# Pooled attention with a gated MLP on one core: a new order of issue for the stretch ahead of the repeated part, and a 1e-9 added by GpSimd

## The chip, the core and the metric

The kernel runs on one core of a Trainium2 chip. The metric is device time in microseconds (us). The kernel before was timed three times: the median is 588.71 us, the lowest 588.38 us and the highest 590.66 us. GB/s and MB are decimal; KB in the table of DMA issues is 1024 bytes.

## The reference

There are 8 batches of 576 rows, 8 heads of 64. Attention runs against keys and values that are pooled by 8 (72 of each), and its output goes into a gated MLP with a spatial gate over the 576 rows.

```python
k_p = k.reshape(B, H, Sp, pool, D).mean(axis=3)      # Sp = 72, pool = 8
v_p = v.reshape(B, H, Sp, pool, D).mean(axis=3)
scores = scale * np.matmul(q, k_p.transpose(0, 1, 3, 2))
scores = scores - np.max(scores, axis=-1, keepdims=True)
attn = np.exp(scores)
attn = attn / (np.sum(attn, axis=-1, keepdims=True) + 1e-09)
x = np.matmul(attn, v_p)                             # heads side by side: 576 x 512
h = gelu(x @ w_in);  u, v = halves of h              # w_in 512 x 1024, tanh form of gelu
v_n = layer_norm(v) * g_ln
gated = u * (einsum('ts,bsd->btd', w_sg, v_n) + b_sg)
out = x + gated @ w_out
```

The weights w_in and w_out arrive as 64-bit floats and are turned into 32-bit ones in the kernel. The large products run as three passes on fp32r halves (high by high, low by high, high by low).

## The kernel before

The work of a batch is cut into steps. A letter names a step, a digit its part, and each step is a generator that issues some instructions and then yields. A token such as `S0+1` advances step S, part 0, of the batch that lies one after the current one, up to its next yield. `PROLOGUE` (lines 23 to 38) is the list of tokens that fills the pipeline, with batches counted from 0. `PERIOD` (lines 39 to 47) is the repeated part: it is emitted for b = 1 to 10 and holds every step once, spread over several batches. `emit` (line 699) walks these lists, so each engine's queue holds its instructions in the order in which the tokens emit them. Lines 710 to 715 then pin that order for each engine. SyncE (SP) issues almost all DMAs, in token order too, and every engine takes its queue strictly in order.

The steps, with the parts that matter here:

- A and B load keys and values of half the heads into `kvraw` (batch 0's values go to `early`), E loads what is left over of both (`left`), C loads the queries of one pair of heads (`early` and `qraw` for batch 0, `qraw` afterwards).
- K pools the keys. For batch 0 TensorE does it, with matmuls by the identity; from batch 1 on VectorE (DVE) does it, with one TENSOR_REDUCE at line 313 per load. K2 pools the left-over rows (`lp`, DVE), transposes on TensorE and writes the block-diagonal `kbd` (ScalarE, lines 343 and 344). P does the same for the values (`vp`, `vb`, `vbh`, `vbl`, `vl`).
- Q turns the queries into `qT`: through TensorE and ScalarE for batch 0, by a DVE STREAM_TRANSPOSE (line 410) later.
- S is the softmax of one pair of heads. TensorE writes the scores to PSUM (`mps` for batch 0, `aps` later, two buffers each); DVE takes the maximum (`nmax`, line 427). From there the softmax has two forms. The short one: ScalarE takes ten exponentials with the bias and the sum in the same instruction (line 444), DVE adds 1e-9 (line 451). The long one, chosen by the tuple `SOFTMAX` at line 75 for six pairs of batches 0 and 1: DVE subtracts the maximum (line 437), ScalarE takes one exponential of all 720 values a row (line 439), DVE sums (line 447) and adds 1e-9 (line 448). Both end with RECIPROCAL (line 454) and a product (line 455) on DVE. GpSimd (POOL) then copies the left-over columns to `el` (line 461).
- T and L transpose the attention weights and the left-over columns (`e`, `el`) and copy them to `ah`, `al` and `lt`; in L the copies for the two halves of the heads alternate between ScalarE (lines 475 and 476) and DVE (line 478). V multiplies by the pooled values, ScalarE writes `x` and `xhl`'s high half (lines 520 and 521), POOL its low half (line 523).
- H and U are the two halves of x @ w_in, W the spatial gate, O the output product, Z the output's transpose and its stores.
- `lv`, `lu`, `lo`, `ls` load the weights; `v`, `u`, `o`, `s` prepare one part of them each. A part of w_in or w_out costs two ScalarE instructions (lines 194 and 195), two of DVE (197 and 198), one of POOL (200), one of ScalarE (203) and one of POOL (205). A part of w_sg costs a transpose on TensorE, a cast on ScalarE and a subtraction on DVE (line 158, `wsl`).

The lines of the long softmax that the change touches, and the end that both forms share:

```python
        if mode:
            yield
            nc.vector.tensor_reduce(out=ssum, in_=e, axis=AX.X, op=ALU.add)
            nc.vector.tensor_scalar(ssum, ssum, 1e-9, None, op0=ALU.add)
        else:
            yield
            nc.vector.tensor_scalar(ssum, ssum, 1e-9, None, op0=ALU.add)

        rec = flat[:, 0:SLOT * NT].rearrange("p (s k) -> p s k", k=SLOT)[:, :, 2 * SP:2 * SP + 2]
        nc.vector.reciprocal(rec, ssum)
```

Of the kernel before, what the change touches and what calls it, by code (L numbers as in the profile page):

```python
# [20 lines left out]


PROLOGUE = """
A0+0 K0+0 A1+0 C0+0 K1+0 E0+0 lv0 K0+0 C1+0 K2+0 K1+0 K2+0 Q0+0 Q1+0 B0+0 C2+0 K2+0 A1+1 Q0+0 v1 v1 v1 S0+0 C3+0 S0+0
v0 Q1+0 S0+0 v0 B1+0 S1+0 S1+0 S1+0 Q2+0 Q3+0 S1+0 S0+0 Q2+0 v1 lv1 S0+0 Q3+0 v0 S2+0 T0+0 ls0 S1+0 v0 A0+1 S2+0 v1
S3+0 K1+1 E0+1 S3+0 T0+0 S2+0 v0 S3+0 S2+0 S3+0 P1+0 B1+1 S1+0 lu0 v3 P0+0 s3 S2+0 S3+0 T1+0 P2+0 v3 S3+0 s1 C0+1 v2
K0+1 T1+0 B0+1 L0+0 L0+0 v3 s3 C1+1 s1 v3 V0+0 K2+1 lo0 s3 V0+0 v2 V1+0 V1+0 s1 s2 T3+0 T2+0 T3+0 s4 v3 T2+0 v2 u1
V0+0 K2+1 P1+1 Q0+1 u1 K2+1 V1+0 v2 P0+1 u1 V3+0 s2 Q1+1 V3+0 V3+0 V2+0 V2+0 S0+1 v2 s2 C3+1 s4 V0+0 u1 S0+1 V3+0
S0+1 S0+1 u0 S1+1 V2+0 s4 lu1 H2+0 C2+1 S1+1 S1+1 u1 S0+1 u0 S1+1 H0+0 T0+1 H2+0 S1+1 H0+0 u3 Q3+1 u0 P2+1 s0 A1+2
V2+0 U1+0 u3 s0 V1+0 u3 s0 S3+1 u3 H1+0 U1+0 u0 Q2+1 H2+0 T0+1 S3+1 H0+0 H4+0 H2+0 u0 T0+1 H2+0 H2+0 H0+0 S2+1 S0+1  # L30
u2 C0+2 H1+0 H4+0 U0+0 S3+1 H1+0 S2+1 S3+1 H4+0 u3 S2+1 H0+0 u2 S2+1 S3+1 u2 U0+0 u2 H3+0 A0+2 H4+0 o1 H0+0 H3+0 S2+1
u2 o0 H1+0 S3+1 U3+0 H4+0 C1+2 H1+0 H3+0 U2+0 S2+1 P2+1 H4+0 H3+0 U3+0 lo1 P2+1 H4+0 o0 S1+1 L0+1 H1+0 H4+0 H3+0 P2+1
L0+1 L0+1 H3+0 L0+1 o0 U2+0 o0 Q0+2 W2+0 T1+1 V0+1 T1+1 o0 W0+0 o1 K0+2 o1 V0+1 o2 o1 T1+1 V1+1 E0+2 T2+1 W2+0 o1
T2+1 o2 W3+0 o2 W0+0 T2+1 o3 o2 o3 o3 V1+1 V2+1 K1+2 T3+1 V1+1 Q1+2 V2+1 T3+1 W1+0 W0+0 K2+2 o3 W2+0 K2+2 W0+0 T3+1
V3+1 W3+0 W1+0 C2+2 W2+0 K2+2 S0+2 V3+1 S1+2 B0+2 W1+0 S0+2 W3+0 Q2+2 W1+0 W3+0 O0+0 B1+2 V1+1 P1+2 P0+2 S1+2 o2 S0+2
V0+1 S1+2 C3+2 O1+0 O0+0 V2+1 S0+2 S0+2 O0+0 Z0+0 V3+1 O1+0 o3 S2+2 S2+2 P2+2 A0+3 O1+0 H2+1 S1+2 O2+0 Z1+0 O2+0 S2+2
A1+3 Q3+2 T0+2 Z0+0 V3+1 O2+0 H2+1 C0+3
""".split()
# [12 lines left out]
def tile_pooled_attn_gmlp(ctx: ExitStack, tc: tile.TileContext, q, k, v, w_in, g_ln, w_sg, b_sg, w_out, out):  # L51
    nc = tc.nc
# [361 lines left out]
    def step_S(b, g):  # L414
# [30 lines left out]
        if mode:  # L445
            yield
            nc.vector.tensor_reduce(out=ssum, in_=e, axis=AX.X, op=ALU.add)
            nc.vector.tensor_scalar(ssum, ssum, 1e-9, None, op0=ALU.add)
        else:
            yield  # L450
            nc.vector.tensor_scalar(ssum, ssum, 1e-9, None, op0=ALU.add)
# [288 lines left out]
```

## Time and profile before

| | value |
|---|---|
| median of 3 runs | 588.71 us (588.38 to 590.66) |
| the profiled execution's own time | 589.3 us |
| its span, first to last instruction | 587.6 us |
| TensorE (PE) busy | 558.1 us (95%) |
| DVE busy | 411.6 us (70%) |
| ScalarE (ACT) busy | 349.2 us (59%) |
| POOL busy | 220.7 us (38%) |
| mean granted TensorE clock | 0.982 |

Busy time is the sum of an engine's instructions; PE's matmuls are pipelined. Idle time is put down to the event that came last before the engine went on. Rows of the timeline give the start in us, the length in us, the engine, line, operation and tiles, and in square brackets how long the engine sat idle ahead of it and who released it.

### The profile page before, as it was taken

What the parts mean: (1) busy time and instruction counts of PE and PEld (TensorE: products, weight loads), DVE (VectorE), ACT (ScalarE), POOL (GpSimd) and SP (SyncE); (2) the same over time, 40 slices, a digit from 0 to 9 for tenths busy, and PEclk for the clock granted to TensorE, in tenths of its full rate; (3) what the DMA queues carried; (4) which work ended last, traced back from release to release, by engine and by line L of the source; (5) the groups of instructions that cost most, each with busy time, mean ns of one, the idle gap of its engine ahead of it and who ended that gap; (6) DMA issues with size and microseconds to landing.
All of it is one profiled execution on the core that took longest, in us unless ns stands there. A gap on an engine that the chain in (4) does not pass through costs nothing.

```text
span 587.6 us, 10312 instructions
## 1 busy us (share of the span) xinstructions
PE 558.1 (95%) x3793; PEld 527.3 (90%) x3793; DVE 411.6 (70%) x562; ACT 349.2 (59%) x981; POOL 220.7 (38%) x295
## 2 busy tenths in 40 slices
PE   4687997999999999999999999999999999999995
PEld 4675886999999989999999989999999989998995
DVE  1688998997758786787758786787758765444434
ACT  1686784797556775577556775577556775412310
POOL 3337366572407032342407032442407032433230
PEclk9699998999999999999999999999999999999998
DMA  8999651453351733124351634125350211021105
GB/s 213 217 225 197 156 130 27 94 101 64 67 106 37 110 63 86 32 59 94 67 105 37 108 67 95 21 57 98 67 105 1 42 21 21 1 42 21 20 1 82
DMA packets 161282, 46.34 MB, mean 79 GB/s; under 512 B 148752, under 2 KB 148752, under 8 KB 161232
## 3 DMA queue, kind: packets, MB, share of 16 engines
q1 hardware_dynamic: 156464, 45.10, 38.6%
q10 hardware_dynamic: 4768, 0.59, 0.7%
q8 instruction: 30, 0.49, 0.4%
q14 instruction: 20, 0.16, 0.1%
HBM read 36.23 MB, written 9.44 MB: 78 GB/s over the span
## 4 chain that ended last, share of the span: by engine, by line
PE 79%; DVE 7%; DMA 7%; SPq 3%; issue 1%; POOL 1%; ACT 1%; DVEq 0%
PE mps L99 65%; PE aps L99 10%; PE aps L133 3%; SPq L153 3%; DMA qraw<-in_q 2%; DMA stage<-in_moe_w_sg 2%; DMA left<-in_v 1%; DMA raw<-in_moe_w_in 1%; DVE kp L313 1%; DMA kvraw<-in_k 1%; DVE top L198 1%; DVE mps L612 1%; DVE qT L410 0%; DVE bst L565 0%; DVE u L614 0%
## 5 line engine op out<-in xcount | busy, mean ns | idle before, releaser
L99 PE MATMUL mps<-xhl,wih 128*128 128x288 f32 x512 | 89.9, 298 | 0.1
L623 POOL TENSOR_TENSOR glo<-u,ghi 128x576 fp32r<-128x576 f32 x32 | 45.2, 1426 | 112.1 <-ACT ghi L621 111.2
L99 PE MATMUL mps<-wih,xhl 128*128 128x512 f32 x256 | 86.6, 404 | 0.1
L99 PEld LDWEIGHTS mps<-xhl,wih 128*128 128x128 f32 x512 | 75.8, 188 | 1.8 <-ACT vg L561 0.3
L444 ACT ACTIVATE e<-aps,nmax 128x72 f32<-128x72 f32 x240 | 73.3, 350 | 0.6 <-DVE nmax L427 0.3
L612 DVE SCALAR_TENSOR_TENSOR mps<-mps,gcol,bbc 128x576 f32<-128x576 f32 x32 | 26.4, 825 | 51.2 <-PE mps L99 51.2
L99 PEld LDWEIGHTS mps<-wih,xhl 128*128 128x128 f32 x256 | 48.8, 190 | 11.0 <-DVE x L655 0.3
L444 ACT ACTIVATION_READ_ACCUMULATOR e<-aps,nmax 128x1 f32 x240 | 56.5, 236 | 0.0
L99 PE MATMUL mps<-wsh,vhh 128*128 128x288 f32 x256 | 56.2, 301 | 0.0
L99 PE MATMUL mps<-wsh,vhl 128*128 128x288 f32 x256 | 55.4, 298 | 0.0
L99 PE MATMUL mps<-xhl,wil 128*128 128x288 f32 x256 | 55.0, 296 | 0.0
L99 PE MATMUL mps<-wsl,vhh 128*128 128x288 f32 x256 | 55.0, 296 | 0.0
L571 DVE TENSOR_SCALAR vg<-vg,mv,rstd 128x512 f32<-128x512 f32 (+1 forms) x40 | 40.4, 1011 | 19.4 <-POOL rstd L569 19.3
L523 POOL TENSOR_TENSOR xhl<-x,xhl 128x576 fp32r<-128x576 f32 x32 | 45.3, 1428 | 21.8 <-ACT xhl L521 21.8
L99 PE MATMUL mps<-ghi,woh 128*128 128x288 f32 x240 | 52.6, 300 | 0.0
L568 POOL TENSOR_TENSOR rstd<-mv,eps 128x1 f32<-128x1 f32 (+1 forms) x40 | 10.8, 271 | 110.3 <-DVE mv L566 100.9
L99 PE MATMUL mps<-glo,woh 128*128 128x288 f32 x240 | 51.4, 295 | 0.1
L99 PE MATMUL mps<-wil,xhl 128*128 128x512 f32 x128 | 51.5, 402 | 0.0
L99 PE MATMUL mps<-ghi,wol 128*128 128x288 f32 x240 | 51.3, 295 | 0.0
L561 ACT ACTIVATE vg<-mps 128x512 f32<-128x512 f32 x32 | 19.1, 597 | 48.4 <-PE mps L99 46.5
L581 POOL TENSOR_TENSOR vhl<-vg,vhh 128x512 fp32r<-128x512 f32 x32 | 42.3, 1324 | 7.8 <-ACT vhh L579 7.7
L621 ACT CAST ghi<-u 128x576 fp32r<-128x576 f32 x32 | 21.4, 673 | 37.7 <-DVE u L614 37.7
(157 smaller groups left out, 1428.0 us busy)
## 6 DMA issues: line engine op xcount, KB each, us to landing
out<-y SPq DMA_DIRECT2D x118, 72.0 KB
kvraw<-in_k SPq DMA_DIRECT2D x32, 256.0 KB
...
kvraw<-in_v SPq DMA_DIRECT2D x28, 256.0 KB
...
```

The lines of the kernel that those rows point to most:

```text
L99: nc.tensor.matmul(o, lhsT, rhs, start=start, stop=stop)
L133: nc.tensor.transpose(ps[:rows, i * P:(i + 1) * P], src(i), ident if i < NT - 1 else swap)
L153: queue.dma_start(o, i)
L444: nc.scalar.activation(e[:, i, h], slots[i][:, h], AF.Exp, bias=nmax[:, i, h:h + 1], **acc)
L523: (nc.vector if b in LO_DVE else nc.gpsimd).tensor_tensor(xhl[:, 1, g], x32[:, g], xhl[:, 0, g].bitcast(F32), op=ALU.subtract)
L561: nc.scalar.activation(vg, o, AF.Gelu_apprx_tanh)
L568: nc.gpsimd.tensor_tensor(rstd, mv[:, 1:2], eps[:n, 1:2], op=ALU.add)
L571: nc.vector.tensor_scalar(vg, vg, mv[:, 0:1], rstd, op0=ALU.subtract, op1=ALU.mult)
L581: (nc.gpsimd if i < NT - 1 else nc.vector).tensor_tensor(lo, vg, hi.bitcast(F32), op=ALU.subtract)
L612: nc.vector.scalar_tensor_tensor(vs, vs, gcol[:, d:d + 1], bbc.rearrange("p (a n) -> p a n", a=2), op0=ALU.mult, op1=ALU.add)
L621: nc.scalar.copy(ghi[:, d], uf)
L623: nc.gpsimd.tensor_tensor(glo[:, d], uf, ghi[:, d].bitcast(F32), op=ALU.subtract)
```

## The change

The diff has two parts.

First, `PROLOGUE` is written anew; `PERIOD` and all steps but one stay as they are. The same steps are emitted, in another order. Its first two lines before and after:

```diff
-A0+0 K0+0 A1+0 C0+0 K1+0 E0+0 lv0 K0+0 C1+0 K2+0 K1+0 K2+0 Q0+0 Q1+0 B0+0 C2+0 K2+0 A1+1 Q0+0 v1 v1 v1 S0+0 C3+0 S0+0
+A1+0 A0+0 lv0 v1 E0+0 v1 K0+0 C0+0 v0 K0+0 K2+0 C1+0 K1+0 C2+0 Q0+0 K1+0 K2+0 Q1+0 v0 Q0+0 K2+0 C3+0 S0+0 v1 v0 lv1
...
```

Second, the long softmax. The pair (0, 1) leaves the tuple and takes the short form, and in the five that remain the 1e-9 is added by POOL from a small constant tile, in a step of its own, so that other work can be put between the sum, the addition and the reciprocal:

```diff
-    SOFTMAX = ((0, 1), (0, 3), (1, 0), (1, 1), (1, 2), (1, 3))
+    SOFTMAX = ((0, 3), (1, 0), (1, 1), (1, 2), (1, 3))
...
+    tiny = const.tile([P, NT, 2], F32, name="tiny")
+    nc.gpsimd.memset(tiny, 1e-9)
...
             nc.vector.tensor_reduce(out=ssum, in_=e, axis=AX.X, op=ALU.add)
-            nc.vector.tensor_scalar(ssum, ssum, 1e-9, None, op0=ALU.add)
+            yield
+            nc.gpsimd.tensor_tensor(ssum, ssum, tiny, op=ALU.add)
+            yield
```

Line numbers below 107 stay, those up to the softmax move by 2, those behind it by 4.

Three places show what the new list does to the queues. The first is SP's queue, from the loads of the spatial gate's bias on; `left`, `kvraw` and `qraw` are batch 1's, `raw` is a weight. Before:

```order
L153 DMA gcol_105<-in_moe_g_ln 128x4x1
L153 DMA kvraw_292<-in_k 64x2x512 x2
L153 DMA left_306<-in_k 32x1x512 x2
L153 DMA left_306<-in_v 32x1x512 x2
L153 DMA kvraw_344<-in_v 64x2x512 x2
L153 DMA raw_349<-in_moe_w_in 128x4x512
L153 DMA qraw_393<-in_q 32x18x32 x4
L153 DMA kvraw_404<-in_v 64x2x512 x2
L153 DMA qraw_417<-in_q 32x18x32 x4
L153 DMA raw_430<-in_moe_w_out 128x4x512
```

SP's queue at the same place after the change:

```order
L155 DMA gcol_107<-in_moe_g_ln 128x4x1
L155 DMA left_265<-in_k 32x1x512 x2
L155 DMA left_265<-in_v 32x1x512 x2
L155 DMA kvraw_292<-in_k 64x2x512 x2
L155 DMA raw_346<-in_moe_w_in 128x4x512
L155 DMA kvraw_358<-in_k 64x2x512 x2
L155 DMA qraw_406<-in_q 32x18x32 x4
L155 DMA qraw_427<-in_q 32x18x32 x4
L155 DMA kvraw_437<-in_v 64x2x512 x2
L155 DMA raw_442<-in_moe_w_out 128x4x512
L155 DMA raw_508<-in_moe_w_in 128x4x512
L155 DMA kvraw_678<-in_v 64x2x512 x2
```

Both loads of batch 1's values stood ahead of its second load of queries and now stand behind it, the second of them behind two more weights. The second load of batch 1's keys, which stood ahead of the spatial gate's weights, now stands behind them.

The second place is DVE's queue where batch 1's first two softmaxes (`e_538`, `e_575`) run. Before:

```order
L427 TENSOR_REDUCE nmax_573<-aps_545 128x10
L437 TENSOR_TENSOR e_575<-aps_545,nmax_573 128x720
L447 TENSOR_REDUCE ssum_539<-e_538 128x10
L448 TENSOR_SCALAR ssum_539<-ssum_539 128x10
L454 RECIPROCAL aps_518<-ssum_539 128x5x2
L455 TENSOR_TENSOR e_538<-e_538,aps_518 128x720
L197 TENSOR_SCALAR top_542<-top_542 128x512
L198 SCALAR_TENSOR_TENSOR top_542<-raw_349,top_542 128x512
L447 TENSOR_REDUCE ssum_576<-e_575 128x10
L448 TENSOR_SCALAR ssum_576<-ssum_576 128x10
L454 RECIPROCAL aps_545<-ssum_576 128x5x2
L455 TENSOR_TENSOR e_575<-e_575,aps_545 128x720
```

DVE's queue at the same place after the change, where the two softmaxes are `e_540` and `e_558`:

```order
L429 TENSOR_REDUCE nmax_554<-aps_543 128x10
L439 TENSOR_TENSOR e_558<-aps_543,nmax_554 128x720
L449 TENSOR_REDUCE ssum_541<-e_540 128x10
L315 TENSOR_REDUCE vp_595<-kvraw_437 128x128
L458 RECIPROCAL aps_532<-ssum_541 128x5x2
L459 TENSOR_TENSOR e_540<-e_540,aps_532 128x720
L449 TENSOR_REDUCE ssum_559<-e_558 128x10
L569 BN_STATS bst_619<-vg_593 128x6
```

The additions are gone from this queue, and a pooling of batch 1's values (`vp`), which stood well ahead of the first softmax, now stands between its sum and its reciprocal. Six rows further on, not shown, comes the second pooling, and the second softmax's reciprocal four rows behind that.

The third place is POOL's queue around the layer-norm instructions (`rstd`) of batch 0's first two parts of H. Before:

```order
L205 TENSOR_TENSOR wil_96<-top_478,wih_95 128x4x128
L200 TENSOR_TENSOR top_542<-top_542,raw_349 128x512
L379 TENSOR_TENSOR left_306<-lp_93,mask_80 32x2x256
L200 TENSOR_TENSOR top_613<-top_613,raw_553 128x512
L568 TENSOR_TENSOR rstd_692<-mv_689,eps_77 128x1
L569 TENSOR_TENSOR rstd_692<-rstd_692,mhalf_75 128x1
L568 TENSOR_TENSOR rstd_703<-mv_700,eps_77 128x1
L569 TENSOR_TENSOR rstd_703<-rstd_703,mhalf_75 128x1
L205 TENSOR_TENSOR wil_96<-top_542,wih_95 128x4x128
```

POOL's queue after the change, with the additions of batch 1's first two softmaxes:

```order
L202 TENSOR_TENSOR top_505<-top_505,raw_346 128x512
L207 TENSOR_TENSOR wil_98<-top_465,wih_97 128x4x128
L451 TENSOR_TENSOR ssum_541<-ssum_541,tiny_80 128x10
L572 TENSOR_TENSOR rstd_623<-mv_620,eps_77 128x1
L573 TENSOR_TENSOR rstd_623<-rstd_623,mhalf_75 128x1
L572 TENSOR_TENSOR rstd_655<-mv_652,eps_77 128x1
L573 TENSOR_TENSOR rstd_655<-rstd_655,mhalf_75 128x1
L451 TENSOR_TENSOR ssum_559<-ssum_559,tiny_80 128x10
L207 TENSOR_TENSOR wil_98<-top_505,wih_97 128x4x128
```

The first addition stands ahead of these layer-norm instructions, the second behind both pairs of them, which wait for DVE's BN_STATS.

More of the change, by code (lines that the diff above doesn't have):

```diff
@@ L23 @@
 PROLOGUE = """
-A0+0 K0+0 A1+0 C0+0 K1+0 E0+0 lv0 K0+0 C1+0 K2+0 K1+0 K2+0 Q0+0 Q1+0 B0+0 C2+0 K2+0 A1+1 Q0+0 v1 v1 v1 S0+0 C3+0 S0+0
[L25 to L37, printed above, removed]
+A1+0 A0+0 lv0 v1 E0+0 v1 K0+0 C0+0 v0 K0+0 K2+0 C1+0 K1+0 C2+0 Q0+0 K1+0 K2+0 Q1+0 v0 Q0+0 K2+0 C3+0 S0+0 v1 v0 lv1
@@ new lines @@
+Q2+0 v1 S0+0 B1+0 B0+0 Q3+0 Q1+0 v1 ls0 S1+0 v0 S1+0 Q2+0 S0+0 E0+1 S1+0 S0+0 S2+0 Q3+0 A0+1 v3 T0+0 S1+0 S2+0 S3+0
+S0+0 v3 S3+0 S3+0 S2+0 P0+0 lu0 v0 S2+0 S3+0 v2 v3 S3+0 A1+1 P1+0 S1+0 S2+0 S3+0 P2+0 T0+0 s3 v3 T1+0 S3+0 S3+0 L0+0
+s3 v3 v2 C0+1 v2 s4 s3 T1+0 K0+1 L0+0 s4 C1+1 V0+0 B0+1 v2 K2+1 lo0 T2+0 s4 s1 V0+0 s1 T2+0 u1 v2 V1+0 V1+0 V2+0 T3+0
+s2 u1 V2+0 K1+1 V0+0 T3+0 K2+1 u0 lu1 K2+1 s2 s1 u1 V3+0 Q0+1 V3+0 u0 Q1+1 s2 V1+0 S0+1 S0+1 S0+1 S1+1 u1 V2+0 V1+0
+V3+0 u0 S1+1 V2+0 S0+1 S1+1 u0 V0+0 H0+0 H2+0 u1 S1+1 S0+1 S0+1 H0+0 P0+1 S0+1 H2+0 S1+1 u3 s0 s0 V3+0 T0+1 H0+0 U1+0
@@ new lines @@
+H2+0 s0 U1+0 S1+1 H1+0 T0+1 u0 B1+1 H0+0 P1+1 C3+1 u3 P2+1 C2+1 H2+0 H0+0 S1+1 S0+1 Q2+1 u2 u2 H2+0 H0+0 Q3+1 H1+0
+P2+1 T0+1 H4+0 P2+1 H4+0 u2 H4+0 S2+1 H3+0 H2+0 S3+1 S2+1 H4+0 S1+1 C1+2 S2+1 u2 u2 u3 C0+2 H1+0 H3+0 S2+1 U0+0 u3
+S3+1 u3 S3+1 S2+1 H4+0 S3+1 H3+0 U0+0 P2+1 o0 H1+0 U2+0 H4+0 S3+1 S2+1 S3+1 S2+1 U3+0 S2+1 lo1 H1+0 S3+1 o1 A1+2 o1
+U2+0 E0+2 H4+0 S3+1 H1+0 L0+1 H3+0 T1+1 H3+0 L0+1 H4+0 L0+1 H3+0 Q0+2 o1 U3+0 W2+0 L0+1 o1 V0+1 o1 o3 o0 T1+1 K1+2
+W2+0 T1+1 o3 W3+0 T2+1 o0 o0 W3+0 o0 V0+1 o2 V1+1 o2 T2+1 o2 T2+1 W0+0 A0+2 V1+1 V2+1 o3 K0+2 o2 W2+0 V1+1 T3+1 B0+2
@@ L38 @@
+W1+0 K2+2 V2+1 W2+0 T3+1 W0+0 W0+0 T3+1 W3+0 o2 K2+2 K2+2 V3+1 C2+2 W0+0 W1+0 W3+0 P0+2 W1+0 W1+0 S0+2 O0+0 S0+2 V1+1
+O1+0 Q2+2 V2+1 V3+1 S0+2 B1+2 A0+3 O0+0 P1+2 Q1+2 S0+2 V3+1 S1+2 O0+0 A1+3 O1+0 P2+2 o3 S1+2 S1+2 S2+2 O2+0 O1+0 S2+2
+C3+2 V0+1 S2+2 Z0+0 O2+0 S1+2 o3 V3+1 Z0+0 H2+1 H2+1 Q3+2 C0+3 O2+0 Z1+0 S0+2 T0+2
 """.split()
```

## The prediction

> **What bounds the kernel now.** I read the page's slices first, then a table of windows over the stretches that the slices set apart, then PE's timeline where it waits, and last what DVE, ACT and the loads do there.
>
> ```profile
> PE   4687997999999999999999999999999999999995
> DVE  1688998997758786787758786787758765444434
> ```
>
> PE has gaps only in the first eight slices of 14.7 us and at the very end; DVE is nearly full from the third slice to the eighth. The windows put numbers to it; the columns are the width, then busy us and count of PE, PEld, DVE, ACT and POOL, the clock, the DMA share and GB/s:
>
> ```profile
> 0.00:57.88 57.88, 39.51 (x231) 34.64 (x232) 34.98 (x42) 34.87 (x95) 25.68 (x46) 0.91 0.96 214
> 57.88:122.02 64.14, 59.49 (x382) 54.90 (x380) 60.69 (x84) 45.32 (x77) 35.00 (x41) 0.95 0.44 98
> 122.02:570.00 447.98, 447.67 (x3099) 426.62 (x3100) 309.37 (x428) 268.31 (x809) 158.47 (x209) 1.00 0.32 59
> ```
>
> From 122.02 us to 570 PE idles 0.31 us of 447.98, at full clock. Nearly all of that is the repeated part, which stays, so whatever comes early or late at 122 us comes so at the end. Ahead of 57.88 us PE idles 18.4 us, with the DMA engines 96% busy; from there to 122 us it idles 4.65 us, with DVE busy 60.69 of 64.14. So there are two terms: when the stretch of H begins, and how much PE loses in it. PE's timeline names the waits at both:
>
> ```profile
> 56.68 1.46 PE L99 MATMUL aps<-kbd,qT 128*128 128x144 f32 x10 [2.38 <-ACT wih L203]
> 57.88 0.64 PE L99 MATMUL mps<-wih,xhl 128*128 128x512 f32 x1
> 98.93 0.49 PE L99 MATMUL aps<-ah,vbh 128*128 128x288 f32 x1 [3.33 <-DVE lt L478]
> ```
>
> The first row is the scores of batch 1's second pair, and batch 0's first H (the second row) follows it; the third is batch 1's first V. The first wait is put down to ACT, but the chain of waits shows whose it is:
>
> ```profile
> 50.87 4.81 DMA qraw<-in_q
> 55.75 0.79 DVE qT L410
> ```
>
> The queries of that pair land at 55.7, DVE transposes them, and PE takes them at 56.68. The loads are the bound here.
>
> **First term: the loads ahead of H.** In SP's new order the queries of batch 1's first two pairs stand ahead of both loads of its values. All else that stood ahead of them still does, in another order. What is taken away, with two windows to price it:
>
> ```profile
> kvraw<-in_v SPq DMA_DIRECT2D x4, 256.0 KB
> 3.50:7.00 3.50, 1.40 (x6) 1.43 (x7) 0.00 (x0) 0.00 (x0) 3.23 (x9) 1.00 1.05 239
> 28.00:31.50 3.50, 3.50 (x20) 3.49 (x19) 2.72 (x2) 1.66 (x9) 1.19 (x3) 0.61 1.03 392
> ```
>
> Two steps of two loads of 256 KB are 1.05 MB. The window from 3.5 to 7 us holds mostly loads of this very shape, at 239 GB/s with the engines full: 1.05 MB is 4.4 us. The bounds are 4.9 us at the 214 GB/s of the whole stretch, and 2.7 us at 392 GB/s. I take 4.4: the queries land at 51.3 and H begins at 53.5 instead of 57.88. [...]
>
> That holds if ACT and DVE are done by then with what follows batch 0's last softmax. Its exponential, its product, the cast of its V, where H's second part goes, and DVE's rows:
>
> ```profile
> 33.61 0.80 ACT L439 ACTIVATE e<-e 128x720 f32<-128x720 f32 x1
> 36.86 0.90 DVE L455 TENSOR_TENSOR e<-e,mps 128x720 f32<-128x720 f32 x1
> 53.91 0.67 ACT L521 CAST xhl<-x 128x576 fp32r<-128x576 f32 x1
> 65.32 0.60 ACT L561 ACTIVATE vg<-mps 128x512 f32<-128x512 f32 x1 [1.23 <-PE mps L99]
> L565 DVE BATCH_NORM_STATS2 bst<-vg 128x6 f32<-128x512 f32 (+1 forms) x5 | 3.4, 672 | 0.7 <-ACT vg L561 0.7
> L313 DVE TENSOR_REDUCE vp<-kvraw 128x128 f32<-128x1024 f32 x4 | 7.9, 1988 | 0.3 <-DMA kvraw<-in_v 0.3
> L410 DVE STREAM_TRANSPOSE qT<-qraw 128x576 f32<-128x576 f32 x7 | 5.4, 774 | 2.0 <-DMA qraw<-in_q 2.0
> L197 DVE TENSOR_SCALAR top<-top 128x512 int32<-128x512 int32 x12 | 6.1, 508 | 2.7 <-ACT top L194 2.7
> L198 DVE SCALAR_TENSOR_TENSOR top<-raw,top 128x512 int32<-128x512 int32 x12 | 10.4, 871 | 0.4
> L235 DVE TENSOR_TENSOR wtl<-mps,wth 64x576 fp32r<-64x576 f32 x1 | 0.7, 740 | 0.0
> ```
>
> On ACT 20.2 us lie between the exponential's end at 34.4 and the cast's at 54.6. The new order has the same work there plus the two casts to `wth`, at 0.67 as the cast above 1.3 us: 55.9, if ACT waits as often. H's first two parts, 24 matmuls, took from 57.88 to 65.3, so 0.31 us each, and the seventh is the first to read this pair: 53.5 + 1.9 = 55.4. On DVE the new order puts 13.8 us between that product and the end of the second `qT`: three poolings (2.0 each), three pairs of weight instructions (1.38), two `wsl` and a `wtl` (0.74 each) and two `qT` (0.77). 37.8 + 13.8 = 51.6, and the loads make it 52.1. Both are just in time, without counting that batch 0's softmax can come sooner.
>
> **What lies under the loads and costs nothing.** The pair (0, 1) in the short form, and the first weight ahead of the left-over rows and the queries:
>
> ```profile
> 20.09 0.32 ACT L444 ACTIVATE e<-mps,nmax 128x72 f32<-128x72 f32 x1 [2.05 <-DVE nmax L427]
> 23.06 0.85 ACT L439 ACTIVATE e<-e 128x720 f32<-128x720 f32 x1
> L437 DVE TENSOR_TENSOR e<-mps,nmax 128x720 f32<-128x720 f32 x2 | 1.8, 908 | 0.1
> L447 DVE TENSOR_REDUCE ssum<-e 128x10 f32<-128x720 f32 x6 | 5.4, 895 | 0.0
> L448 DVE TENSOR_SCALAR ssum<-ssum 128x10 f32<-128x10 f32 x6 | 3.7, 616 | 0.2
> L451 DVE TENSOR_SCALAR ssum<-ssum 128x10 f32<-128x10 f32 x2 | 0.3, 175 | 0.3 <-ACT e L444 0.3
> ```
>
> Ten short exponentials run from 20.09 to 23.06, so the short form puts 2.97 - 0.85 = 2.1 us on ACT and takes 0.91 + 0.90 + (0.62 - 0.18) = 2.2 us from DVE. Both lie ahead of 57.88 us, where DVE idles 22.9 us and ACT 23.0; the cover is the loads, and the cost without it is the 2.1 us on batch 0's chain.
>
> **Second term: DVE's queue from H to the first V.** L448 and L451 are the same addition. It takes 175 ns where POOL is quiet and 616 on the mean in the long form. Between the first maximum of batch 1 and the last `lt`, the new queue has two more poolings of values, one more `qT`, one pair of weight instructions and one `wtl` less, and four additions less. What DVE waited for between the two `lt`:
>
> ```profile
> 98.03 0.75 DVE L478 TENSOR_TENSOR lt<-aps,lt 32x576 fp32r<-32x576 f32 x1 [1.33 <-ACT lt L476]
> ```
>
> That is 2 x 1.99 + 0.77 - 0.51 - 0.87 - 0.74 - 4 x 0.62 = +0.2 us. The `qT` now stands between the two `lt`, in the 1.33 us that DVE waited there, so 0.8 us of it are free: -0.6 us in all. Against this stands the second pooling, whose load is now behind two weights: 0.52 + 1.05 + 1.05 + 0.52 = 3.15 MB after 51.3 us, landing at 64.5 at 239 GB/s and at 66.0 at 214. DVE starts the first maximum at 52.9 (transpose and `wsl` behind 51.3) and reaches that pooling about 11.7 us later, at 64.6: seven softmax rows of 0.9, a pooling, two statistics of 0.67 and `wsl` are 10.4, and for the small rows between them and one normalization I add 1.3, an estimate. So it waits 0 to 1.4 us, and I take 0.7. The term is +0.1 us.
>
> The additions on POOL, not seen in this trace, are nearest to these rows:
>
> ```profile
> L568 POOL TENSOR_TENSOR rstd<-mv,eps 128x1 f32<-128x1 f32 (+1 forms) x5 | 1.2, 246 | 4.8 <-DVE mv L566 4.8
> L523 POOL TENSOR_TENSOR xhl<-x,xhl 128x576 fp32r<-128x576 f32 x6 | 8.5, 1419 | 0.0
> ```
>
> One costs POOL 0.25 us, and at worst stands behind a subtraction of 1.42 that has just begun. A reciprocal that waits holds all of DVE's queue. For the first pair of batch 1 a pooling of 1.99 us covers the addition, for the second a pooling and five more rows, for the fourth the third's reciprocal and product (1.1 us). For batch 0's last pair nothing stands between, but that lies under the loads. I take 0; at worst two of them stick out by 1.42, 2.8 us. [...]
>
> **The sum.** -4.4 + 0.1 = -4.3 us: 589.3 of the profiled execution becomes 585.0, and as its time stands 0.6 above the median of 588.71, the forecast is 584.4 us. Its own range is from 580.5 (4.9 at H, and the gap at V closed) to 587.4 (2.7 at H, and 1.4 at the pooling); the additions at their worst alone make 587.2. A change under about 0.5%, 2.9 us, can't be told from none.
>
> **Rivals.** First, the gap at V closes as well. DVE instructions ahead of `lt` are stretched while POOL works, and PE then runs at a lower clock:
>
> ```profile
> 92.53 1.68 DVE L581 TENSOR_TENSOR vht<-vg,vht 64x512 fp32r<-64x512 f32 x1
> 94.23 1.68 DVE L393 TENSOR_TENSOR vl<-left,vl 32x512 fp32r<-32x512 f32 x1
> 101.85 0.69 PE L99 MATMUL mps<-wsh,vhl 128*128 128x288 f32 x2
> 102.92 0.43 PE L99 MATMUL mps<-wsh,vhl 128*128 128x288 f32 x2
> ```
>
> `vl` now stands some twelve rows ahead of `lt`. If the 3.33 us go, and with them the slow clock from 98.93 to 102.3 (half of 3.4 us), the sum is -4.4 - 3.3 - 1.7 = -9.4: 579.3 us. For it: DVE had 22.9 us free ahead of H. Against: its queue up to `lt` is no shorter. 0.20.
>
> Second, no change that can be told: the gain at H is given back at the second pooling. The loads there ran at 186 GB/s in one window:
>
> ```profile
> 60.00:70.00 10.00, 10.00 (x57) 8.66 (x56) 9.69 (x17) 7.05 (x13) 3.05 (x3) 0.93 0.73 186
> ```
>
> Then the load lands at 51.3 + 16.9 = 68.2, DVE waits 3.6 us instead of 0.7, and the sum is -1.4: 587.3 us. It decides from about 2 us of wait on. Against: the engines were only 73% busy in that window. 0.16.
>
> Third, slower: batch 0's softmax becomes the bound. Now its left-over rows and queries load behind the first weight (4.4 us), and ACT prepares that weight ahead of copying batch 0's pooled keys:
>
> ```profile
> L194 ACT ACTIVATE top<-raw 128x512 f32<-128x512 f32 x5 | 3.4, 676 | 0.1
> L195 ACT ACTIVATE raw<-raw 128x512 int32<-128x512 uint32 x5 | 3.3, 663 | 0.0
> 25.09 1.19 PE L403 MATMUL aps<-ident,qraw 96*128 96x96 f32 x6 [3.51 <-DMA qraw<-in_q]
> ```
>
> Two parts are 2.7 us, and with the 2.1 of the short form the last product ends 9.2 us late, at 47.0. DVE's 13.8 us behind it end at 60.8 instead of the 56.5 at which the second `qT` ended, and H begins 4.3 us later than before: 593.0 us. It decides once that product is late by more than 4.9 us. Against: DVE idles 22.9 us ahead of H, and the last queries of batch 0, which PE waited for until 25.09, now load ahead of the second weight and of all values. 0.11.
>
> **How the numbers follow.** The forecast has 0.53; faster by over 0.5% is 0.50 of it and the first rival, 0.70; within 0.5% the rest of it and the second, 0.19; slower 0.11. The range from 578.5 to 588.5 holds the first rival with 4.9 us at H (578.8) and the second down to no gain at all; it leaves out the third.
>
> **What would show it.** Right: batch 1's second `qT` ends near 52, the first H starts near 53.5, the gap ahead of V stays at 2 to 4 us, and no reciprocal waits over 0.5 us for POOL. A first H at 57 or later would make the first term wrong, a gap at V under 1 us the second; a stall of DVE at a `vp` names the second rival, a last product of batch 0 behind 42.7 us the third. PE idle over 1 us behind the last O of batch 0 would break the step that carries the gain to the end.

## The result, and the profile after

| | before | after |
|---|---|---|
| median | 588.88 us (11 runs, 585.77 to 590.66) | 584.10 us (11 runs, 582.48 to 586.86) |
| the profiled execution's own time | 589.3 us | 584.24 us |
| its span | 587.6 us | 582.5 us |

The ratio after to before is 0.9929, with a 95% interval from 0.9913 to 0.9946: the change made the kernel 0.7% faster, and the interval leaves out 1. The forecast was 584.4 us. (Two executions among the experiments, one of before with 911 us and a granted clock of 0.56 and the profiled one of the last run with 0.66, are in no comparison.)

In the page of after, in slices of 14.6 us, PE first reaches 9 in the third slice (the fifth before) and DVE in the fourth (the fifth before):

```profile
PE   3698988999999999999999999999999999999995
DVE  0579998988668795778667785688667765344434
```

The windows are cut at the same events as before: the first H, the first V of batch 1, and the stretch behind it.

```profile
0.00:53.30 53.30, 36.95 (x231) 31.58 (x232) 30.15 (x40) 38.01 (x116) 25.56 (x47) 0.97 0.88 215
53.30:93.50 40.20, 35.63 (x223) 31.29 (x222) 37.78 (x56) 28.74 (x47) 24.75 (x36) 1.00 0.54 137
...
118.55:570.00 451.45, 450.84 (x3124) 429.43 (x3123) 307.93 (x429) 267.07 (x796) 154.06 (x206) 1.00 0.32 58
```

H begins at 53.30 instead of 57.88 (4.58 us earlier) and V at 93.50 instead of 98.93 (5.43 earlier); the span is 5.1 us shorter. From the start of V to the end of the span it is 489.0 us after and was 488.7 before: what is gained by V stays to within 0.3 us. PE loses 0.6 us in the 451 us of the third row.

The timeline of after shows what each engine waited for on the way:

```profile
34.84 0.91 DVE L459 TENSOR_TENSOR e<-e,mps 128x720 f32<-128x720 f32 x1
...
40.19 1.98 DVE L315 TENSOR_REDUCE kp<-kvraw 128x128 f32<-128x1024 f32 x1 [2.67 <-DMA kvraw<-in_k]
...
51.19 0.77 DVE L412 STREAM_TRANSPOSE qT<-qraw 128x576 f32<-128x576 f32 x1
52.10 1.46 PE L99 MATMUL aps<-kbd,qT 128*128 128x144 f32 x10 [0.21 <-DVE qT L412]
53.30 0.49 PE L99 MATMUL mps<-wih,xhl 128*128 128x512 f32 x1
...
63.32 2.04 DVE L315 TENSOR_REDUCE vp<-kvraw 128x128 f32<-128x1024 f32 x1
...
86.76 0.63 PE L135 MATMUL aps<-ident,el 128*64 128x128 f32 x4 [1.39 <-POOL el L465]
92.61 0.75 DVE L482 TENSOR_TENSOR lt<-aps,lt 32x576 fp32r<-32x576 f32 x1 [0.53 <-ACT lt L480]
93.50 0.37 PE L99 MATMUL aps<-ah,vbh 128*128 128x288 f32 x1 [1.69 <-DVE lt L482]
```

Batch 0's last product ends at 35.75 (37.76 before). DVE then waits 2.67 us for the first load of batch 1's keys and runs from 40.19 without a pause to the end of the second `qT` at 51.96. The second pooling of values at 63.32 waits for nothing. The gap ahead of V is 1.69 us (3.33 before).

### The profile page after: what moved, and what is told of

Read it like the earlier page. It is cut to its first block, busy times and chain, and to the rows that moved or that the text cites. A ratio compares the mean times of both kernels' runs of the same rounds, so it can differ in the third digit from the quotient of the medians.

```text
span 582.5 us, 10319 instructions
## 1 busy us (share of the span) xinstructions
PE 554.7 (95%) x3793; PEld 522.9 (90%) x3793; DVE 405.6 (70%) x555; ACT 351.9 (60%) x1000; POOL 222.7 (38%) x301
## 4 chain that ended last, share of the span: by engine, by line
PE 79%; DVE 10%; ACT 4%; DMA 3%; SPq 2%; issue 1%; ACTq 0%; POOL 0%; DVEq 0%
PE mps L99 65%; PE aps L99 11%; PE aps L135 3%; ACT e L446 2%; SPq L155 2%; DMA left<-in_v 1%; DMA qraw<-in_q 1%; DVE e L459 1%; DVE bst L569 1%; DVE nmax L429 1%; DVE vg L575 1%; DVE vp L315 1%; DMA out<-y 1%; DVE ssum L449 1%; DVE qT L412 1%
```

## The experiments

All times are read from the profiled execution of each kernel, medians and ratios from all its runs. Each ratio is to runs of before taken alongside, whose medians were 588.5 to 588.9 us. Every kernel is told by the same five events; "product" is the end of batch 0's last product on DVE, "qT" the end of the second `qT` of batch 1.

| run | product | qT | H starts | V starts | H to V | median | ratio to before, interval |
|---|---|---|---|---|---|---|---|
| before | 37.76 | 56.53 | 57.88 | 98.93 | 41.05 | 588.88 | |
| after | 35.75 | 51.96 | 53.30 | 93.50 | 40.20 | 584.10 | 0.9929 (0.9913 to 0.9946) |
| before, value loads late | 38.67 | 51.25 | 53.80 | 98.54 | 44.74 | 589.85 | 1.0026 (1.0011 to 1.0042) |
| before, poolings late | 37.32 | 55.05 | 56.45 | 101.25 | 44.80 | 591.55 | 1.0075 (1.0046 to 1.0104) |
| after, a value load early | 34.83 | 50.62 | 51.97 | 92.16 | 40.19 | 583.39 | 0.9918 (0.9898 to 0.9938) |
| after, queries of batch 0 late | 42.65 | 57.29 | 58.64 | 98.84 | 40.20 | 589.59 | 1.0025 (1.0010 to 1.0040) |
| after, keys early | 35.53 | 50.84 | 52.19 | 94.49 | 42.30 | 584.03 | 0.9928 (0.9904 to 0.9953) |
| after, addition on DVE | 35.90 | 51.95 | 53.30 | 93.88 | 40.58 | 584.91 | 0.9939 (0.9919 to 0.9959) |
| after, (0, 1) long | 36.20 | 52.19 | 53.54 | 93.93 | 40.39 | 584.50 | 0.9928 (0.9902 to 0.9953) |
| before, softmax part | 44.34 | 59.93 | 61.28 | 102.37 | 41.09 | 592.23 | 1.0073 (1.0050 to 1.0096) |
| before, additions on POOL | 39.50 | 59.07 | 61.44 | 102.24 | 40.80 | 591.68 | 1.0047 (1.0028 to 1.0066) |
| after, vbl early | 34.83 | 50.59 | 51.94 | 90.52 | 38.58 | 582.62 | 0.9913 (0.9892 to 0.9934) |
| the same, bias late | 34.96 | 49.62 | 50.97 | 89.55 | 38.58 | 581.27 | 0.9864 (0.9842 to 0.9886) |

In all of them the span ends 488.0 to 490.6 us behind the start of V. A profile's early part shifts by 1.1 to 1.4 us from execution to execution (the products of after and of its variants with the same early part end between 34.8 and 35.9, those of before and its first two variants between 37.3 and 38.7), so a difference of H of that size is not read by itself; the column from H to V repeats much closer.

**The value loads moved alone.** Before, with the loads of batch 1's values behind its queries, and their poolings on DVE behind the first softmax rows:

```diff
-S2+0 S3+0 P1+0 B1+1 S1+0 ... T1+0 B0+1 L0+0 ... s3 C1+1 s1 ... K2+1 P1+1 Q0+1 ... v2 P0+1 u1
+S2+0 S3+0 P1+0 S1+0 ... T1+0 L0+0 ... s3 C1+1 B0+1 B1+1 s1 ... K2+1 Q0+1 ... v2 u1
...
-S1+1 S1+1 u1 S0+1 u0 S1+1 H0+0 T0+1 H2+0 S1+1 H0+0
+S1+1 S1+1 P0+1 u1 S0+1 u0 S1+1 H0+0 T0+1 H2+0 S1+1 P1+1 H0+0
```

> The kernel before, with its softmax and its order, except that both loads of batch 1's values stand behind the queries of its second pair on SP, and their two poolings stand behind the first two maxima and subtractions on DVE, where the values have landed. PE's, ACT's and POOL's orders are those of before. Theory: the loads set when H begins, so the second qT ends near 52 and H begins near 53.5 (57.88 before); but DVE's queue from the first maximum to the last lt gets two poolings longer, 4.0 us, and the gap ahead of V grows from 3.3 to 6 to 7.5 us: the time is 588 to 589, no change against 588.9, and the load order alone is worth nothing without what the change takes from DVE's queue elsewhere. Rival (the prediction's first term read alone): the start of H carries through, 584.4. Second rival: DVE is not ready at 51, H stays at 56 or later and the time rises above 589.

Its timeline:

```profile
50.48 0.77 DVE L410 STREAM_TRANSPOSE qT<-qraw 128x576 f32<-128x576 f32 x1
53.80 0.49 PE L99 MATMUL mps<-wih,xhl 128*128 128x512 f32 x1
98.54 0.37 PE L99 MATMUL aps<-ah,vbh 128*128 128x288 f32 x1 [3.34 <-DVE lt L478]
```

The theory held in the main: H begins 4.1 us earlier, and the stretch from H to V grows by 3.7 us, so V begins 0.4 us earlier only and no time is gained (589.85 us, 0.3% above before and above the forecast 588 to 589). The gap ahead of V, forecast to grow to 6 to 7.5 us, stayed at 3.34; the loss lies in PE's waits ahead of it, the longest two for DVE (1.74 us at 61.42 and 1.53 at 67.72). Behind H the two poolings cost nearly all of their 4 us.

**The poolings moved alone**, the loads where before has them:

```diff
-K2+1 P1+1 Q0+1 ... v2 P0+1 u1
+K2+1 Q0+1 ... v2 u1
...
-S1+1 S1+1 u1 S0+1 u0 S1+1 H0+0 T0+1 H2+0 S1+1 H0+0
+S1+1 S1+1 P0+1 u1 S0+1 u0 S1+1 H0+0 T0+1 H2+0 S1+1 P1+1 H0+0
```

> The kernel before, with only the two poolings of batch 1's values moved on DVE behind the first two maxima and subtractions, as in the run that also moved their loads; SP's order is that of before, the values load ahead of the second pair's queries. Theory (in before the queries' landing at 55.7 us sets the second qT): DVE waits for them instead of pooling, H stays at 57 to 57.9, the 4.0 us of poolings come on top behind it, V starts at 101 to 102.5, and the time is 591 to 593. Rival (the order of the loads hardly counts, DVE's queue set the start of H all along): H begins near 53.8 and the time is that of the run with both moves, 589 to 590.

```profile
49.95 0.78 DVE L410 STREAM_TRANSPOSE qT<-qraw 128x576 f32<-128x576 f32 x1 [2.63 <-DMA qraw<-in_q]
54.27 0.78 DVE L410 STREAM_TRANSPOSE qT<-qraw 128x576 f32<-128x576 f32 x1 [2.51 <-DMA qraw<-in_q]
56.45 0.49 PE L99 MATMUL mps<-wih,xhl 128*128 128x512 f32 x1
101.25 0.58 PE L99 MATMUL aps<-ah,vbh 128*128 128x288 f32 x1 [3.33 <-DVE lt L478]
```

DVE now waits for each pair's queries: with the values ahead of them the queries' landing does set the second `qT`, at 54.27. H comes 2.65 us later than with the loads moved too, and the 4 us of poolings come on top. (It comes 1.4 us earlier than in before, and 0.55 ahead of the theory's 57 to 57.9: the queries land at 54.2 here and landed at 55.7 there.)

**One value load put back** in after, between the two loads of queries:

```diff
-K0+1 L0+0 s4 C1+1 V0+0 B0+1 v2
+K0+1 B0+1 L0+0 s4 C1+1 V0+0 v2
```

> The kernel after, with one change on SP: the first load of batch 1's values stands between the two loads of queries again (0.52 MB ahead of the second pair's queries); all other queues as they are. Theory A (the prediction's first term: the queries' landing sets the second qT): they land 2.2 us later at 239 GB/s, the second qT ends near 54.1, H begins near 55.5 and the time is 586.3. Theory B (DVE's queue behind the load of the keys sets it, the queries had landed with time to spare): part of the 2.2 us is hidden; if all of it, H stays at 53.3 and the time at 584.1. Halfway, 585, would put the slack of the queries at about 1 us.

The timeline of this run, and from its chain of waits the load of the second pair's queries:

```profile
49.85 0.77 DVE L412 STREAM_TRANSPOSE qT<-qraw 128x576 f32<-128x576 f32 x1
51.97 0.49 PE L99 MATMUL mps<-wih,xhl 128*128 128x512 f32 x1
```

```profile
47.21 2.41 DMA qraw<-in_q
```

Theory B: nothing is lost. The queries land at 49.62 and DVE takes them at 49.85, without a recorded wait. So in after the queries had time to spare for that load, an estimated 2.2 us (0.52 MB at 239 GB/s): with only the second value load behind the queries the time is the same.

**Batch 0's queries put back** in after: half of batch 0's values ahead of the queries of its third pair, half of batch 1's keys ahead of those of its fourth, as before has them:

```diff
-C1+0 K1+0 C2+0 ... K2+0 C3+0 S0+0 ... B1+0 B0+0 Q3+0 ... S3+0 A1+1 P1+0
+C1+0 K1+0 B0+0 C2+0 ... K2+0 A1+1 C3+0 S0+0 ... B1+0 Q3+0 ... S3+0 P1+0
```

> The kernel after, with two loads put back on SP to where before had them: half of batch 0's values stands ahead of the queries of its third pair, and half of batch 1's keys ahead of those of its fourth; all other queues as they are. In the traces batch 0's last product on DVE ended at 37.8 us in before and at 34.8 to 35.9 in after and its three variants. Theory: that is worth 2 us of the gain, and it comes from those queries, for which PE waited 3.51 us in before and not at all in after. With 0.52 and 1.05 MB ahead of them again they land 2.2 and 4.4 us later, the last product ends at 37 to 38, the start of H and of V move with it, and the time is 585.5 to 586.5. Rival A: DVE's wait of 2.67 us for batch 1's keys at 40.2 takes it up, H stays near 53.3 and the time at 584. Rival B: the queries had so much time to spare that the last product stays below 36.3, and the time at 584.

```profile
25.70 1.20 PE L405 MATMUL aps<-ident,qraw 96*128 96x96 f32 x6 [3.16 <-DMA qraw<-in_q]
29.34 0.91 DVE L429 TENSOR_REDUCE nmax<-mps 128x10 f32<-128x720 f32 x1 [9.26 <-PE mps L99]
...
41.75 0.90 DVE L459 TENSOR_TENSOR e<-e,mps 128x720 f32<-128x720 f32 x1
58.64 0.49 PE L99 MATMUL mps<-wih,xhl 128*128 128x512 f32 x1
98.84 0.37 PE L99 MATMUL aps<-ah,vbh 128*128 128x288 f32 x1 [1.70 <-DVE lt L482]
```

The whole gain is gone, and more than the theory priced: the last product ends 6.9 us late, not 2. In the new order the transposes of batch 0's last queries stand ahead of the scores of its second pair on PE (`Q3+0` ahead of `S1+0`), so all of them wait for the last load: DVE sat 9.26 us ahead of the second maximum. Of the 6.9 us DVE's wait for batch 1's keys took up 2.2 (it is 0.43 here), a wait of 0.66 for ACT came on top, and H comes 5.3 us later. From H to V it is 40.20 us, as in after to the hundredth.

**The keys early** in after:

```diff
-Q1+0 v1 ls0 S1+0 ... Q3+0 A0+1 v3
+Q1+0 v1 A0+1 ls0 S1+0 ... Q3+0 v3
```

> The kernel after, with one change on SP: the first load of batch 1's keys stands ahead of the spatial gate's weights and not behind them; all other queues as they are. In the trace of after DVE waited 2.67 us for that load at 40.2 us and then ran without a pause to the end of the second qT at 51.96. Theory (DVE's queue behind that load sets the start of H, the queries have landed by then): the wait shrinks by about 2 us, the second qT ends near 50, H begins at 51.3 to 52, and the time is 582 to 583. Rival A (the prediction's first term: the loads of the queries set it): DVE waits for the queries instead, H stays at 53.3 and the time at 584.1. Rival B: the gate's weights, 2.2 us later, hold PE's transposes and so H: 585 to 586.

```profile
43.80 0.43 DVE L199 TENSOR_SCALAR top<-top 128x512 int32<-128x512 int32 x1 [1.51 <-ACT top L196]
52.19 0.49 PE L99 MATMUL mps<-wih,xhl 128*128 128x512 f32 x1
62.85 0.76 DVE L160 TENSOR_TENSOR wsl<-mps,wsh 128x576 fp32r<-128x576 f32 x1 [1.65 <-ACT wsh L158]
94.49 0.37 PE L99 MATMUL aps<-ah,vbh 128*128 128x288 f32 x1 [1.71 <-DVE lt L482]
```

The wait of 2.67 us for the keys is gone, but DVE now waits 1.51 us for ACT at 43.80, and H begins only 1.1 us earlier, no more than the shift between executions. Behind it DVE waits another 1.65 us for ACT, the stretch to V grows by 2.1 us, and the time is that of after. That is rival A's time, but not for its reason: DVE waited for no queries. The gate's weights, 2.2 us later by estimate, are a likely cause of the second wait, which is for a part of them (`wsh`); that was not followed further.

**The addition back on DVE** in after, at the same place in the order:

```diff
-            nc.gpsimd.tensor_tensor(ssum, ssum, tiny, op=ALU.add)
+            nc.vector.tensor_scalar(ssum, ssum, 1e-9, None, op0=ALU.add)
```

> The kernel after, but the 1e-9 of the five long softmaxes is added by DVE again, at the very place in the order where POOL added it. Theory (the prediction's second term: the additions weighed on a full DVE): four of them stand between batch 1's first maximum and the last lt; at the 0.62 us that was the mean of the long form's rows before they cost 2.5 us, at the four rows of batch 1 themselves (0.17, 0.67, 0.65, 0.47) 2.0 us. DVE idles only 1.7 us in that stretch, so the gap ahead of the first V of batch 1 grows from 1.7 to 3.5 to 4 us and the time from 584.1 to about 586.3. Rival A: an addition costs DVE 0.175 us as in the short form, 0.7 us in all: 584.8. Rival B: the handing over to POOL and back costs as much as the addition: no difference that can be told, 583.7 to 584.6.

```profile
33.64 1.03 POOL L381 TENSOR_TENSOR vl<-lp,mask 32x512 f32<-32x512 f32 x1
33.90 0.80 DVE L451 TENSOR_SCALAR ssum<-ssum 128x10 f32<-128x10 f32 x1
56.95 0.17 DVE L451 TENSOR_SCALAR ssum<-ssum 128x10 f32<-128x10 f32 x1
63.10 0.17 DVE L451 TENSOR_SCALAR ssum<-ssum 128x10 f32<-128x10 f32 x1
84.08 0.28 DVE L451 TENSOR_SCALAR ssum<-ssum 128x10 f32<-128x10 f32 x2
93.88 0.37 PE L99 MATMUL aps<-ah,vbh 128*128 128x288 f32 x1 [1.69 <-DVE lt L482]
```

Rival A: at most 0.17 us each for batch 1, and the stretch from H to V grows by 0.38 us. The time differs by 0.8 us, within the intervals. Only the one of batch 0's last pair, at 33.90, beside which a POOL operation runs from 33.64 to 34.67, takes 0.80. By the instruction DVE is the quicker here (0.17 us against 0.21 to 0.47 on POOL in after); yet on a DVE that is the bound the move to POOL still took 0.38 us off the stretch. In the order of before, where POOL was often at work, the same additions had taken up to 0.67 us in batch 1; the first two of the four:

```profile
62.19 0.17 DVE L448 TENSOR_SCALAR ssum<-ssum 128x10 f32<-128x10 f32 x1
65.47 0.67 DVE L448 TENSOR_SCALAR ssum<-ssum 128x10 f32<-128x10 f32 x1
```

**The pair (0, 1) long** in after:

```diff
-    SOFTMAX = ((0, 3), (1, 0), (1, 1), (1, 2), (1, 3))
+    SOFTMAX = ((0, 1), (0, 3), (1, 0), (1, 1), (1, 2), (1, 3))
...
-E0+1 S1+0 S0+0 ... T0+0 S1+0 S2+0
+E0+1 S1+0 S1+0 S0+0 ... T0+0 S1+0 S1+0 S1+0 S2+0
```

> The kernel after with the pair (0, 1) in the long form again (its addition on POOL like the others'; three more tokens of that step in the list, SP's queue as it is). The short form puts 2.1 us on ACT and takes 2.2 us from DVE; in the trace of after DVE waited 1.11 and 1.66 us for the exponentials of batch 0's first two pairs. Theory (the prediction: it lies under the loads either way): batch 0's last product ends up to 1 us earlier or later than the 34.8 to 35.9 of after and its variants, DVE's wait of 2.67 us for batch 1's keys at 40 us takes that up, and the time is 583.3 to 584.8. Rival A: the short form is worth its 2.2 us of DVE, 586. Rival B: the short form costs its 2.1 us of ACT on batch 0's chain, 582.

584.5 us, with every event within 0.5 us of after. The theory held: in the new order the form of that pair makes no difference that can be told.

**The softmax part alone**, in the order of before, with the constant `tiny` as in after:

```diff
-    SOFTMAX = ((0, 1), (0, 3), (1, 0), (1, 1), (1, 2), (1, 3))
+    SOFTMAX = ((0, 3), (1, 0), (1, 1), (1, 2), (1, 3))
...
-            nc.vector.tensor_scalar(ssum, ssum, 1e-9, None, op0=ALU.add)
+            nc.gpsimd.tensor_tensor(ssum, ssum, tiny, op=ALU.add)
```

> The order of issue of before, with the softmax part of the change alone: the pair (0, 1) in the short form, and in the five long ones POOL adds the 1e-9 directly between DVE's sum and reciprocal, with no work in between. Theory: DVE loses four additions of batch 1 (0.17, 0.67, 0.65 and 0.47 us, 2.0 in all) and gains four waits for POOL, each at least the 0.32 us that the reciprocal of (0, 3) waited in after, longer where POOL is inside a subtraction of 1.3 us, which the rows of 0.47 to 0.67 say it often is: 1.3 to 3 us of waits. Net 0 to +1 us at the gap ahead of V, time 588.5 to 590: the softmax part alone is worth nothing. Rival A: the additions are worth their 2 us even so, 587. Rival B: the short form of (0, 1) makes batch 0's last product 1 to 2 us earlier or later than 37.8 and H moves with it: 587 or 590.

The stretch from H to V is 41.09 us against 41.05, as the theory said. But H begins 3.4 us late, and the kernel is 0.7% slower. These are the events of rival B, with a larger price; the next run tests its reason.

**The additions alone on POOL**, in the order of before and with all six long forms (the second half of the diff above):

> The order of issue of before with all six long softmaxes of before; the only change is that POOL adds the 1e-9, directly between DVE's sum and reciprocal. In the run with the whole softmax part in that order H began 3.4 us later than before, at 61.28, and the stretch from there to V was as long as before (41.1 us). Theory: the handing over to POOL costs DVE about what the addition cost it (waits of 0.32 to 0.73 us against additions of 0.17 to 0.67), so batch 0's last product ends within 0.7 us of 37.8, H begins within 1 us of 57.9, and the time is 588 to 589.5; the 3.7 us of that other run then belong to the short form of the pair (0, 1) in an order that was not made for it. Rival: the POOL additions themselves delay batch 0's chain, H begins near 61 and the time is 591.5 to 592.5.

The timeline of this run:

```profile
65.90 0.22 DVE L456 RECIPROCAL aps<-ssum 128x10 f32<-128x10 f32 x1 [0.32 <-POOL ssum L450]
...
88.52 0.22 DVE L456 RECIPROCAL aps<-ssum 128x10 f32<-128x10 f32 x1 [0.72 <-POOL ssum L450]
```

The theory was wrong and the rival's numbers came: H at 61.44, 591.7 us. Not by the mechanism that either gave, though. The four waits for POOL in batch 1 are 0.32 three times and 0.72 once, 1.7 us against the 2.0 of the additions, and from H to V it is 40.80 us. The two in batch 0 are 1.13 and 0.32, against additions of 0.93 and 0.80. And the pair (0, 1) is long here, so its short form is not the reason either. What is late are the loads, and long before the first addition: from 7 to 14 us, with the loads issued in the same order, before moved 269 GB/s and this run 239; the softmax part alone moved 233, the two runs with moved value loads 268 and 267. The window of before, then that of this run:

```profile
7.00:14.00 7.00, 5.74 (x37) 5.31 (x35) 1.88 (x1) 0.85 (x4) 0.00 (x0) 1.00 0.96 269
```

```profile
7.00:14.00 7.00, 5.48 (x30) 5.05 (x29) 1.51 (x1) 0.53 (x2) 0.00 (x0) 1.00 0.95 239
```

The first long softmax runs at 24 us. Two things of the softmax part lie ahead of that: the memset of the new constant, and its place in memory, which puts every buffer behind it 64 bytes further on. The last run below tried the second.

**vbl early** in after. The two subtractions to `vbl` took 2.56 us in after and 0.82 in before. In after two POOL operations ran beside them; the first reads the `top` that the weight pair ahead of `vbl` writes, and starts at 70.29, just after that pair ends at 70.15. The subtractions now stand ahead of that pair:

```diff
-S0+1 Q2+1 u2 u2 ... Q3+1 H1+0 P2+1 T0+1
+S0+1 Q2+1 P2+1 u2 u2 ... Q3+1 H1+0 T0+1
```

> The kernel after, with one step moved on DVE alone: the two subtractions to vbl, which took 2.56 us for two while POOL ran two operations beside them (0.82 in before, where POOL was quiet), stand four rows earlier, ahead of the weight pair that releases POOL's next operation; all other queues as they are. Theory (DVE's queue from the first maximum to the last lt sets the start of V, and the stretched rows in it are a matter of meeting POOL): vbl takes about 0.8 us, everything behind it on DVE comes up to 1.7 us earlier, the gaps of 1.39 us ahead of the transposes of el and 1.69 us ahead of V shrink by as much in sum, and the time is 582.3 to 583. Rival A: another DVE instruction meets POOL's operations in its place and the time stays at 584.1. Rival B: V is set by ACT's copies to lt and not by DVE's queue: the gap moves from one place to the other, 584.1.

The timelines of after and of this run at that place:

```profile
70.29 1.31 POOL L202 TENSOR_TENSOR top<-top,raw 128x512 int32<-128x512 int32 x1 [1.76 <-issue]
70.76 2.56 DVE L388 SCALAR_TENSOR_TENSOR vbl<-vp,vbh 64x256 fp32r<-64x256 f32 x2
71.55 1.49 POOL L585 TENSOR_TENSOR vhl<-vg,vhh 128x512 fp32r<-128x512 f32 x1
```

```profile
67.78 0.83 DVE L388 SCALAR_TENSOR_TENSOR vbl<-vp,vbh 64x256 fp32r<-64x256 f32 x2
83.77 0.63 PE L135 MATMUL aps<-ident,el 128*64 128x128 f32 x4 [0.76 <-POOL el L465]
90.52 0.37 PE L99 MATMUL aps<-ah,vbh 128*128 128x288 f32 x1 [1.69 <-DVE lt L482]
```

The theory held: `vbl` takes 0.83, and from H to V it is 38.58 us, 1.62 less than in after. Two DVE instructions moved by three rows (the pair and one `qT`) are worth four times what the four additions are (0.38 us). The gaps do not shrink by as much as the theory said: the one at V stays at 1.69, the one ahead of `el` falls from 1.39 to 0.76, and one of 0.72 us for DVE at 74.17 is gone. The time is 1.5 us below that of after, but the intervals of the two ratios overlap; it is the stretch from H to V that shows the gain.

**The bias late**: on top of this, the spatial gate's bias and gain load behind batch 1's queries, by a step of their own (`lb0`):

```diff
+    def load_bias():
         load(bbc, b_sg.rearrange("(o t) -> o t", o=1).broadcast_to([P, S]))
         load(gcol, g_ln.rearrange("(c p) -> p c", p=P))
...
-u3 P2+1 C2+1 H2+0
+u3 P2+1 C2+1 lb0 H2+0
```

> The kernel with vbl early (582.6 us), and on SP the two loads of the spatial gate's bias and gain (0.3 MB for the bias, broadcast to all partitions, and many small pieces for the gain), first used near 87 us, stand behind batch 1's queries and not ahead of its left-over rows and keys. Theory (DVE's queue behind the load of batch 1's keys, for which it waited 2.15 us at 38.75, sets the start of H): the keys land 1.3 us or more earlier (0.3 MB at 239 GB/s), DVE's wait shrinks by as much, H begins 1 to 2 us earlier and the time is 580.8 to 581.8. Rival A: behind DVE's wait ACT's work or PE's is late by then, as in the run with the keys ahead of the gate's weights, and the gain is given back before V: 582.6. Rival B: the late loads themselves make W wait: above 583.

Vbl early, and then this run:

```profile
38.75 1.98 DVE L315 TENSOR_REDUCE kp<-kvraw 128x128 f32<-128x1024 f32 x1 [2.15 <-DMA kvraw<-in_k]
```

```profile
37.59 1.96 DVE L317 TENSOR_REDUCE kp<-kvraw 128x128 f32<-128x1024 f32 x1 [0.85 <-DMA kvraw<-in_k]
50.97 0.49 PE L99 MATMUL mps<-wih,xhl 128*128 128x512 f32 x1
89.55 0.37 PE L99 MATMUL aps<-ah,vbh 128*128 128x288 f32 x1 [1.71 <-DVE lt L484]
```

As the theory said: the keys come 1.2 us earlier, DVE's wait shrinks by 1.3, H and V both begin 1.0 us earlier, and the time is 581.3 us. The products of the two runs end within 0.13 us of each other, so this is not the shift between executions. This version beats both kernels, before by 1.4% (1.1 to 1.6).

**The addresses of before**: the same, with the new constant in a tile of 512 bytes a partition:

```diff
-    tiny = const.tile([P, NT, 2], F32, name="tiny")
+    tiny = const.tile([P, P], F32, name="tiny")[:, 0:2 * NT].rearrange("p (t h) -> p t h", h=2)
```

> The run with the bias loaded late (581.3 us), with one change in memory: the 40 bytes a partition of the new constant lie in a tile of 512 bytes, so that every buffer behind it starts at the same place within 512 bytes as in before, and no longer 64 bytes further on; orders and instructions are the same. In the two runs that have the loads of before in the order of before but the new constant in memory, the loads moved 233 and 239 GB/s from 7 to 14 us against 267 to 269 in before and its two other variants, and H began 3.4 to 3.6 us late. Theory A (the 64 bytes slow the loads): from 7 to 14 us the loads move 260 GB/s or more against 247, batch 0's last product ends before 34.5 (34.96), H begins 0.5 to 2 us before 50.97, and the time is 579 to 580.7; then the change itself carries a cost of that size, and the delay of those two runs isn't the handing over to POOL. Theory B (where the buffers lie does not matter, and the handing over or the short form slowed those two runs): 245 to 250 GB/s, H within 0.4 us of 50.97, and the time 580.8 to 581.8.

This settles nothing: three of its runs took 578.9 to 579.3 us, about as theory A had it, and three 581.1 to 582.9, about as theory B had it; the ratio to before is 0.9863 (0.9835 to 0.9890), that of the run without it. No profile of it can be set beside the others. What slowed the loads of the two runs in the old order stays open.

## Why the prediction was right, step by step

**The loads ahead of H (-4.4 us; measured -4.58).** The size came out, and the events as well: the second `qT` was forecast to end near 52 and ended at 51.96, H near 53.5 and came at 53.30. The reason was half of it, and so the fit of the size is partly luck. That the queries' landing bound H in before is shown by the run with the poolings moved alone. But in after it no longer did: with one value load put back the queries, forecast to land at 51.3 without it, landed at 49.62, and nothing was lost. What bound there is the second condition, which the prediction counted as just in time: DVE's 13.8 us of work behind batch 0's last product. Without the wait for the keys it took 51.96 - 35.75 - 2.67 = 13.5 us; it could begin 2.0 us earlier than before, and lost all of that again to the keys. It ended at 51.96, where the price of the loads had put it (52.1), for another reason. So the step needs three loads in time, not one: the queries of batch 1, its keys, and the queries of batch 0. The last count most: put back, they took the whole gain. The prediction had them only as an argument against its third rival.

**That the first term carries through.** It did, to within 0.3 us: from V to the end it is 489.0 us against 488.7, and PE idles 0.6 us in the stretch behind 118.55 us. But the run with the value loads moved alone shows that it would not have by itself: the poolings that leave the stretch ahead of H come into the one behind it, and 4.1 us at H were 0.4 us at V. The change keeps its gain because its new order took about as much from DVE's queue there as the poolings added, as the second term reckoned.

**DVE's queue from H to V (+0.1 us; measured -0.85).** The sum came within 1 us, but its parts did not come out, so this too is partly luck. Mis-sized: the four additions, taken at 0.62 us each, 2.5 in all. They had cost 2.0 in before, where POOL was at work beside three of the four; at their new places the same instruction costs 0.17, and having it on POOL is worth 0.38. That no reciprocal of batch 1 would wait for POOL came true. The wait for the second pooling, 0.7 forecast, was nil. Left out: which instructions would meet POOL. `vbl` grew from 0.82 to 2.56, while `vht` and `vl`, 1.68 each in before, fell to 0.69 and 0.68. These three changes of 1.0 to 1.7 us nearly cancel; the run with `vbl` early shows that the first counts almost in full (1.62 us), and the other two were not tried. PE's part was also unforeseen: the granted clock was 1.00 from H to V in after, but since DVE bounds the stretch, it is V's start that counts and not PE's pace.

**The sum.** Between the profiled executions it is -4.58 - 0.85 + 0.3 = -5.1 us, between the medians -4.8, against the forecast -4.3. The prediction's own range of 580.5 to 587.4 leaves out the -0.6 us with which its second term begins; with it the range is 579.9 to 586.8.

**What lies under the loads.** The short form of (0, 1) costs and brings nothing in the new order, as forecast. The first weight ahead of the left-over rows was not tried by itself.

**The rivals.** The gap at V did not close (1.69, not under 1), though it fell short of the 2 to 4 us that the prediction expected. The slow clock behind V stayed as well: 0.60 over the first 3.4 us in after, 0.51 in before. The second pooling waited for nothing, so the second rival fell. The third named a bound that is real: it was to decide once the last product ends 4.9 us late, at 42.7 us. In the run with batch 0's queries late it ended at 42.65, and H began at 58.64, 0.8 us behind that of before. That it didn't happen in after is due to the loads that the prediction set against it.
